# Trading two slots of a streaming ring for two more kept tiles in a two-layer decode kernel

## The chip, the cores and the metric

The kernel runs on one core of one Trainium2 chip; the other cores are idle. The metric is the time of one execution in microseconds (us) as the device measures it. Executions of one kernel agree within about 0.3% for the kernel before and within about 1% for some of the variants below. Ratios are computed as the mean time of one kernel's fast runs over the mean time of the other's fast runs of the same rounds, so they are not quite the ratio of the medians that are quoted.

Engine names are those of the profile: PE (matmul), PEld (PE's weight loads), DVE, ACT, POOL and SP, which issues the DMAs.

## The reference, cut to what matters

Two identical layers with the same weights and the same caches act on a batch of 8 single tokens. Each layer is an attention over a cache of 4096 positions (8 key/value heads, 256 wide, two query heads on each) and then a small MLP block.

```python
q = (layernorm(x) @ wq)                      # 8 tokens, 16 query heads of 256
scores = einsum(q, k_cache) / 16             # k_cache, v_cache: [8, 8, 4096, 256] bf16
o = softmax(scores) @ v_cache
x = x + o @ wo
x = x + B(layernorm(x))                      # gelu MLP, w3: 448 x 1792, w4: 1792 x 448
# ... and the same once more, with the same caches
```

Both caches together are 2 x 128 MiB. Each layer needs all of them, while all that the kernel holds on chip comes to about 26 MiB (206.9 KiB in each of 128 partitions, counted from the code). So nearly every byte has to be streamed twice.

## The kernel before: what the change and the argument touch

The caches are streamed in half tiles of 1 MiB (2048 positions of one head) through a ring of slots, always in the order in which they are used:

```python
N_RING = 6                 # slots of 8 KiB a partition
N_KEEP = 8                 # half tiles of transposed keys that stay, 8 KiB a partition each
...
def load_next():
    n = state["loaded"]
    ...
    t, r = ring[n % N_RING]
    op("sp", lambda e: e.dma_start(t[:, :, :], ...), writes=[r], dma=f"ring{n % N_RING}")
```

`op` records an operation with what it reads and writes and works out the waits: a load waits until the last reader of its slot is done. A keys half tile is turned (16 transposes on PE, evicted by DVE or ACT), and its slot is free then. A values half tile is used by 16 matmuls, after the softmax.

The turned keys of layer 1 can be **kept** on chip. With `N_KEEP = 8`, four of eight heads of a token keep theirs, so layer 2 has to stream only their values. The kept tiles serve one token at a time, so layer 2 of token b runs interleaved with layer 1 of token b + 1:

```python
full = N_KEEP // 2
kept_heads = full + N_KEEP % 2
A  = lambda b: [(0, b, h) for h in range(kept_heads, HKV)]   # layer 1, not kept
Bk = lambda b: [(0, b, h) for h in range(kept_heads)]        # layer 1, kept
C  = lambda b: [(1, b, h) for h in range(kept_heads)]        # layer 2, keys on chip
Dn = lambda b: [(1, b, h) for h in range(kept_heads, HKV)]   # layer 2, all streamed
...
per = (len(first) + len(second)) / B        # first: all A of tokens 1..7, second: all Dn of 0..6
...
for b in range(B):
    ... # about `per` heads out of first and second: the streaming stage S_b
    for i in range(kept_heads):             # the mixed stage M_b
        seq += C(b)[i:i + 1]
        if b + 1 < B:
            seq += Bk(b + 1)[i:i + 1]
```

Between the last kept head of token b in layer 1 (end of stage M) and its first kept head in layer 2 (start of the next M) lies the token's **chain**: output projection, layernorm, MLP, another layernorm, new queries. It has about 370 small matmuls in 46 steps on PE, and some 30 steps on other engines, which depend on each other. The chain is fed into the program in pieces, one or so at each of the 14 **pump** calls of a streamed head; what is left when the first kept head comes is drained at once:

```python
def step():
    ...                                     # records the next piece of the first job
    return 1.0 if len(S.ops["pe"]) > n else 0.4   # 1.0 for a piece with PE work

def pump():
    credit["n"] = min(1.0, credit["n"] + credit["rate"]) if jobs else 0.0
    if credit["n"] > 0.0:
        credit["n"] -= step()
...
    if layer == 0:                          # a token's last head of layer 1 is done
        credit["rate"] = 0.80
        jobs.append(mix(b, 1, True))        # its chain
...
for g, (layer, b, h) in enumerate(seq):
    if layer == 1 and all(s_[:2] != (1, b) for s_ in seq[:g]):
        drain()                             # the chain must be over before layer 2 of token b
    w = attend(g)
```

So a round of the pipeline is: streaming stage S (7 heads of four 1 MiB transfers, with the chain), mixed stage M (four pairs of six transfers, no chain).

## Time and profile before

Two runs: 1195.41 and 1197.05 us, median 1196.23. (The profiled execution is another one, of 1198.42 us.)

These are lines of the page of the kernel before. The digits are 40 equal slices of the span: granted PE clock and DMA busy share in tenths, and GB/s. Then come the shares of the chain that ended last, and the ring's transfers with their number, size and median us from issue to landing.

```profile
span 1196.6 us, 42443 instructions
...
PEclk8879989899999998999989899998999999899886
DMA  9999999999999999999999999999999999999992
GB/s 352 388 412 420 419 416 415 420 419 418 417 421 412 415 403 419 420 419 400 409 420 419 414 401 420 418 421 398 410 420 420 418 407 420 420 419 408 397 393 92
...
DMA 44%; PE 39%; DVE 10%; issue 5%; POOL 1%; ACT 1%; SPq 0%; POOLq 0%; ACTq 0%
...
ring<-in_A_v_cache_dram SPq DMA_DIRECT2D x256, 1024.0 KB, 12.7
ring<-in_A_k_cache_dram SPq DMA_DIRECT2D x192, 1024.0 KB, 12.4
```

The DMA line is full from start to the last slice, and the rate stays near 420 GB/s: the kernel is bound by its stream. A transfer needs 12.5 us to land because it queues behind about four others (12.5 / 2.48 us between landings is 5 under way); the ring is nearly always fully asked for.

The stages can be found in the trace, since each head has exactly one maximum over its scores (a TENSOR_REDUCE into `pm`), in the order of the program; a stage ends with its last head's. These are two rows of the stretch view of the kernel before, for the second streaming stage S1 and the mixed stage M1 (start:end, length, then busy us and number of instructions of each engine, granted clock, DMA share, GB/s):

```profile
core 0: us, PE busy (x) PEld busy (x) DVE busy (x) ACT busy (x) POOL busy (x), PEclk, DMA share, GB/s
244.00:315.90 71.90, 62.12 (x1288) 54.55 (x1280) 34.24 (x127) 21.40 (x57) 6.06 (x16) 1.00 1.01 418
315.90:376.10 60.20, 44.17 (x920) 38.29 (x912) 20.65 (x65) 15.42 (x48) 6.02 (x16) 0.94 1.01 416
```

PE is busy 62 of 72 us in S1, and 44 of 60 in M1: the chain makes S the tight stage for PE, while the stream runs at the same rate in both. And these are lines of the view of waits (engine and line, what it waited for: us in total, times, longest) for PE:

```profile
PE tk L574 <- DMA ring<-in_A_k_cache_dram: 120.4, 81, 6.7
PE ps L598 <- DVE sm L324: 17.6, 20, 1.1
PE mm L405 <- DVE t L364: 13.1, 8, 5.0
PE mm L405 <- DVE lnT L364: 9.1, 1, 9.1
```

PE waits for keys (`tk` is the transposition) more than five times longer than for the layernorms' results (L364 writes them, 13.1 + 9.1 us; the 9.1 us is one wait at the start, for the first queries).

| kernel before | value |
|---|---|
| transfers of 1 MiB | 448 |
| median time between two landings | 2.48 us (423 GB/s) |
| streaming stages S0 to S7, sum | 597.1 us (56 heads; 4 x 2.48 us each would be 555.5) |
| mixed stages M0 to M6, sum | 403.8 us (28 pairs; 6 x 2.48 us each would be 416.6) |

Read the last two rows together: in S, PE falls a little behind the stream and the slots fill with landed data; in M, PE catches up by working off what has landed, so an M takes less than its own transfers' time.

### The profile page before, as it was taken

How to read it: one execution, taken by the hardware profiler on the slowest of the kernel's cores; microseconds unless marked ns; L12 is line 12 of the kernel's file. 1: busy time of each engine (PE TensorE's matmuls, PEld its weight loads, DVE VectorE, ACT ScalarE, POOL GpSimd, SP SyncE). 2: the span in 40 equal slices, each digit the busy share in tenths (PEclk: the TensorE clock that was granted, in tenths of full speed). 3: DMA queues.
4: the chain of work that ended last, by engine and by line, in shares of the span. 5: the costliest groups of instructions: out<-in, count | busy, mean ns of one | idle time of the engine just before them, and what ended most of it. 6: DMA issues, size and time to landing. Idle time of an engine off the chain costs nothing.

```text
span 1196.6 us, 42443 instructions
## 1 busy us (share of the span) xinstructions
PE 963.4 (81%) x19195; PEld 842.2 (70%) x19195; DVE 485.2 (41%) x1707; ACT 320.9 (27%) x907; POOL 104.9 (9%) x281
## 2 busy tenths in 40 slices
PE   2767898788877888788977897788878897789895
PEld 2666787677766777677866886677767786678784
DVE  2323443335433443335433443335433443345253
ACT  1222322232222222232322322222322232223130
POOL 0000001101011001100110001000110011000100
PEclk8879989899999998999989899998999999899886
DMA  9999999999999999999999999999999999999992
GB/s 352 388 412 420 419 416 415 420 419 418 417 421 412 415 403 419 420 419 400 409 420 419 414 401 420 418 421 398 410 420 420 418 407 420 420 419 408 397 393 92
DMA packets 71828, 483.06 MB, mean 404 GB/s; under 512 B 7376, under 2 KB 13408, under 8 KB 13920
## 3 DMA queue, kind: packets, MB, share of 16 engines
q1 hardware_dynamic: 71648, 480.36, 97.9%
q8 instruction: 150, 2.46, 0.8%
q14 instruction: 30, 0.25, 0.0%
HBM read 480.32 MB, written 0.01 MB: 401 GB/s over the span
## 4 chain that ended last, share of the span: by engine, by line
DMA 44%; PE 39%; DVE 10%; issue 5%; POOL 1%; ACT 1%; SPq 0%; POOLq 0%; ACTq 0%
DMA ring<-in_A_k_cache_dram 44%; PE tk L574 21%; PE ps L598 6%; PE pvb L672 4%; PE mm L405 4%; DVE ktr L581 3%; PE mm L485 2%; PE mm L435 1%; PE pvb L690 1%; DVE sm L343 1%; ACT ktr L579 1%; DVE sm L325 1%; POOL gm L648 1%; DVE sm L326 1%; DVE ob L678 1%
## 5 line engine op out<-in xcount | busy, mean ns | idle before, releaser
L574 PE MATMUL tk<-ident,ring 128*128 128x128 f32 x3072 | 458.3, 298 | 121.9 <-DMA ring<-in_A_k_cache_dram 120.4
L574 PEld LDWEIGHTS tk<-ident,ring 128*128 128x128 f32 x3072 | 368.1, 152 | 160.4 <-DMA ring<-in_A_k_cache_dram 147.9
L581 DVE COPY ktr<-tk 128x512 f32<-128x512 f32 x256 | 176.7, 690 | 258.3 <-PE tk L574 257.6
L579 ACT COPY ktr<-tk 128x512 f32<-128x512 f32 x256 | 148.3, 586 | 358.3 <-PE tk L574 358.2
L672 PE MATMUL pvb<-ring,pT 128*2 128x256 bf16 x4096 | 161.7, 279 | 35.9 <-DMA ring<-in_A_v_cache_dram 28.5
L598 PE MATMUL ps<-qT,ktr 128*128 128x48 bf16 x4096 | 145.4, 184 | 22.6 <-DVE sm L324 17.6
L598 PEld LDWEIGHTS ps<-qT,ktr 128*128 128x128 bf16 x4096 | 130.5, 97 | 34.1 <-DVE ktr L581 26.0
L581 DVE COPY keep<-tk 128x512 f32<-128x512 f32 x128 | 88.5, 691 | 155.3 <-PE tk L574 154.7
L654 ACT ACTIVATE pT<-ps,nb 128x32 bf16<-128x32 f32 x256 | 76.4, 298 | 259.3 <-DVE nb L650 212.0
L598 PE MATMUL ps<-qT,keep 128*128 128x48 bf16 x4096 | 139.6, 186 | 5.1 <-issue 4.4
L598 PEld LDWEIGHTS ps<-qT,keep 128*128 128x128 bf16 x4096 | 130.4, 99 | 18.2 <-issue 10.3
L579 ACT COPY keep<-tk 128x512 f32<-128x512 f32 x128 | 75.0, 586 | 232.5 <-PE tk L574 232.5
L672 PEld LDWEIGHTS pvb<-ring,pT 128*2 128x2 bf16 x4096 | 76.0, 82 | 61.0 <-DMA ring<-in_A_v_cache_dram 35.2
L648 POOL PARTITION_ALL_REDUCE gm<-pm x128 | 45.4, 355 | 778.3 <-DVE pm L645 778.3
L678 DVE COPY ob<-pvb 128x256 f32<-128x256 f32 x128 | 53.7, 419 | 46.9 <-PE pvb L672 46.3
L659 POOL PARTITION_ALL_REDUCE dn<-rs x128 | 51.0, 399 | 150.9 <-ACT pT L654 150.9
L645 DVE TENSOR_REDUCE pm<-ps 128x2 f32<-128x64 f32 x128 | 28.6, 224 | 87.8 <-PE ps L598 87.8
L435 PE MATMUL mm<-oT,wo_sb 128*128 128x24 bf16 (+5 forms) x1280 | 60.6, 183 | 1.4 <-DVE oT L697 0.5
L435 PEld LDWEIGHTS mm<-oT,wo_sb 128*128 128x128 bf16 (+1 forms) x1280 | 51.3, 102 | 12.6 <-issue 9.1
L690 PE MATMUL pvb<-ident,ob 128*128 128x128 f32 x256 | 55.8, 302 | 2.8 <-DVE ob L678 1.6
L405 PE MATMUL mm<-lnT,wq_sb 128*128 128x24 bf16 x864 | 48.6, 184 | 10.5 <-DVE lnT L364 9.1
L405 PEld LDWEIGHTS mm<-lnT,wq_sb 128*128 128x128 bf16 x864 | 42.0, 99 | 19.2 <-DVE lnT L364 10.5
(65 smaller groups left out, 474.7 us busy)
## 6 DMA issues: line engine op xcount, KB each, us to landing
ring<-in_A_v_cache_dram SPq DMA_DIRECT2D x256, 1024.0 KB, 12.7
ring<-in_A_k_cache_dram SPq DMA_DIRECT2D x192, 1024.0 KB, 12.4
wo_sb<-in_A_wo_dram SPq DMA_DIRECT2D x1, 3584.0 KB, 26.8
wq_sb<-in_A_wq_dram SPq DMA_DIRECT2D x3, 1024.0 KB, 11.5
w_sb<-in_B_w_dram SPq DMA_DIRECT2D x1, 1568.0 KB, 22.8
w_sb<-in_B_w_dram SPq DMA_DIRECT2D x3, 448.0 KB, 14.3
wqf_sb<-in_A_wq_dram SPq DMA_DIRECT2D x2, 256.0 KB, 15.2
w3f_sb<-in_B_w_dram SPq DMA_DIRECT2D x2, 112.0 KB, 15.3
```

The costliest lines, as they stand in the source:

```text
L405: last = e.matmul(room(P, at + t * B, n), cols(kc, t), copies(rhs, n), start=(kc == 1), stop=(kc == 0), skip_group_check=True)
L435: last = e.matmul(room(w, at, n) if alone else mm[0:w, at:at + n], wo[:, t, row0(c):row0(c) + w], copies(cols, n) if alone else cols, star ...
L574: last = e.transpose(bank[:, j * P:(j + 1) * P], src[:, 4 * (f % 4) + j, :].bitcast(f32), ident4[:, :])
L579: op("act", lambda e: e.copy(flat, bank[:, :]), reads=[r_bank], writes=[r_kt])
L581: op("dve", lambda e: e.tensor_copy(flat, bank[:, :]), reads=[r_bank], writes=[r_kt])
L598: last = e.matmul(pst[:, at:at + 2 * N_REP].rearrange("p (r j) -> p r j", j=2), kt(i, c), repeated(qT[:, b, c, 2 * h:2 * h + 2]), start=(c ...
L648: op("pool", lambda e: e.partition_all_reduce(gm[q][0][:, :], pm[q][0][:, :], P, ReduceOp.max), reads=[pm[q][1]], writes=[gm[q][1]])
L654: return e.activation(pT[q][0][:, :, :].rearrange("p i j -> p j i")[:, j, :], pst[:, C_S:C_S + 2 * NI].rearrange("p (i j) -> p j i", j=2)[ ...
L659: op("pool", lambda e: e.partition_all_reduce(dn[q][0][:, :], rs[q][0][:, :], P, ReduceOp.add), reads=[rs[q][1]], writes=[dn[q][1]])
L672: last = e.matmul(pvb[at:at + 2, 0:DH], pT[q][0][:, a * HALF + i, :], v[:, i, :], start=(a == 0 and i < 4), stop=(a == 1 and i >= HALF - 4 ...
L678: op("dve", lambda e: e.tensor_copy(ob[:, :], pvb[:, 0:DH]), reads=[r_pv], writes=[r_ob])
L690: last = e.transpose(pvb[:, DH + c * P:DH + (c + 1) * P], ob[:, c * P:(c + 1) * P], ident4[:, :])
```

## The change

Its intent is to stream less. Ten half tiles are kept instead of eight, so five heads of eight stream only values in layer 2: 16 key transfers of 448 go away. The memory for it comes from the ring, which shrinks from six slots to four. With five kept heads there are fewer streaming heads a round (`per` falls from 7 to 5.25), so the chain has to fit in 5 or 6 heads; the pump is made denser for it. This is the whole diff:

```diff
-N_RING = 6
+N_RING = 4
 N_KTR = 4
 N_TK = 4
-N_KEEP = 8
+N_KEEP = 10
 N_REP = 24
 N_MLP = 24
+CHAIN = 60
@@ pump
         credit["n"] = min(1.0, credit["n"] + credit["rate"]) if jobs else 0.0
-        if credit["n"] > 0.0:
+        while credit["n"] > 0.0:
             credit["n"] -= step()
@@ after
         if layer == 0:
-            credit["rate"] = 0.80
+            credit["rate"] = CHAIN / (14 * (per - 1))
             jobs.append(mix(b, 1, True))
```

The rate becomes 60 / (14 x 4.25) = 1.008. With `if`, a step of 0.4 (no PE work) takes a pump of its own; with `while`, up to three of them go into one.

## The prediction

> **What bounds the kernel now.** The DMA stream. The page shows the DMA line at 9 tenths in nearly every slice, 480 MB read from HBM, and 404 GB/s over the span; PE is busy 81%. From the issue and landing times of the 448 ring transfers (1 MiB each), one lands every 2.48 us (423 GB/s) whether 2 or 6 are outstanding; about 17 times an interval grows by 1 to 1.5 us, when a few instruction-fetch packets of the second queue come in (about 27 us in all). The Trainium skill, "HBM Reference", section Specifications, gives about 425 GB/s for one core streaming alone, bounded by its 16 DMA engines; the trace agrees, so no rate is left to gain, only bytes. The DMA is busy without a hole from 3 us to about 1140 us; the tail after the last landing (1176 us) is 20 us.
>
> **What the change does.** Two more half tiles kept: 16 fewer K transfers (192 -> 176), 432 instead of 448: 16 x 2.48 = 39.7 us of stream. It also removes 256 transposes (a half tile's 16 take 2.0 us warm, 3.6 cold) and their evictions, off the critical path. Instruction fetches stay. Pure DMA floor: 1196.2 - 39.7 = about 1156.5 us.
>
> **What is given back.**
> 1. Streaming stages. Between the mixed stages the kernel streams 7 heads (K and V), later 5 or 6, and must run the token's dense chain (about 370 matmuls) there. The head-by-head timeline gives: a streamed head without chain, PE-bound, 7.0 us (the last head), against 4 x 2.48 = 9.9 us of DMA; with chain 9.4 to 11 us. So already now PE is a little slower than DMA there, and outstanding transfers fall from 5-6 to 3-4 in each such stage. After, the chain starts in the second of 5 heads. Estimate for the remaining four: 28 + 12 (370 x 33 ns, read from heads with and without chain) + 4 to 9 us of stalls = 44 to 49 us, against 39.7 us of DMA. Stalls now are about 4.5 us a stage (waits for the layernorm's VectorE results); the `while` lets up to three layernorm steps go in one pump, so their latency is covered by fewer transposes: stalls grow.
> 2. Four slots. Waiting PE leaves about 3.3 transfers outstanding instead of 5.3; PE may fall behind by about 5.5 us before the DMA runs dry, against 10 us. So I expect 1 to 4 us of DMA hole in each of six 5-head stages, about none in the two 6-head ones: 10 us (0 to 24).
> 3. Start: during the first projection two fewer chunks are prefetched: 3 us. The last stages, where only 2 or 3 are outstanding now: 2 us.
>
> The mixed stages (PE idle 12 us of 58 on DMA) stay DMA-bound and get longer: 10 heads, about 75 us.
>
> **Prediction.** 1156.5 + 15 = about 1171 us, 8 in 10 between 1157 and 1188. Faster by over 2%: 0.53; within 2%: 0.44; slower: 0.03.
>
> **What would show the steps.** HBM read near 463.5 MB; K transfers x176; time to landing from 12.5 down to about 7.5 us; landing interval still 2.48 us; in the streaming stages GB/s falls from 407-418 to about 390-405 with moments of no transfer outstanding; the page's GB/s line dips there and stays 420 in mixed stages; waits of PE on VectorE's layernorm lines grow, waits on K transfers shrink.
>
> **What would make it wrong.** If the ring absorbs the chain, 1157-1160. If landing intervals stretch with 1 or 2 outstanding, or the denser chain stalls VectorE's evictions, holes of over 5 us a stage eat the whole gain.

## The result

Two runs: 1287.52 and 1294.52 us, median 1291.02, against 1196.23 before. The ratio is 1.079, 95% interval 1.066 to 1.092: slower by 8%. The prediction had been 1171 us, between 1157 and 1188.

The page of the kernel after, the same lines:

```profile
span 1285.7 us, 41851 instructions
...
PEclk8879888898988988898888987898887988889986
DMA  7999989998999989998999989997999989999893
GB/s 278 370 401 406 361 310 408 404 402 304 393 396 393 356 341 402 394 386 318 376 398 400 359 335 396 400 394 283 394 393 377 368 309 386 375 396 335 335 346 128
...
PE 47%; DMA 39%; DVE 8%; issue 4%; POOL 1%; ACT 0%; SPq 0%; POOLq 0%; ACTq 0%
...
ring<-in_A_v_cache_dram SPq DMA_DIRECT2D x256, 1024.0 KB, 8.3
ring<-in_A_k_cache_dram SPq DMA_DIRECT2D x176, 1024.0 KB, 8.0
```

The 16 key transfers are gone, but the GB/s line now has a deep dip in every round (310, 304, 341, 318 ...), and between the dips it reaches about 400, not 420. PE leads the chain that ended last. The stretch view of the same two stages of the kernel after (S1 now has 5 heads, M1 five pairs):

```profile
262.00:324.50 62.50, 49.64 (x1000) 43.64 (x992) 27.25 (x105) 15.65 (x41) 4.57 (x12) 0.92 0.90 353
324.50:401.90 77.40, 58.54 (x1180) 50.84 (x1172) 26.12 (x82) 19.30 (x60) 7.54 (x20) 0.89 0.99 398
```

S1 takes 62.5 us for 5 heads, whose 20 transfers need 49.6. At 353 instead of 418 GB/s the stage moved 22.1 MB where 26.1 were possible: 9.7 us of stream lost. M1 runs at 398 instead of 416 GB/s, another 3.3 us lost, although PE has 19 us to spare in it. And the view of waits:

```profile
PE tk L575 <- DMA ring<-in_A_k_cache_dram: 142.8, 79, 7.2
PE mm L406 <- DVE lnT L365: 40.1, 10, 11.1
PE mm L406 <- DVE t L365: 31.1, 9, 5.0
PE mm L486 <- DVE hT L477: 9.2, 10, 1.2
```

PE now waits 71 us for the layernorms' results (40.1 + 31.1) where it waited 22 (9.1 + 13.1), and it waits longer for keys too.

| | before | after |
|---|---|---|
| transfers | 448 | 432 |
| S0 to S7, sum | 597.1 us, 56 heads | 528.5 us, 42 heads (4 x 2.48 us each: 416.6) |
| M0 to M6, sum | 403.8 us, 28 pairs | 551.2 us, 35 pairs (6 x 2.48 us each: 520.8) |
| first 8 heads | 110.3 us | 119.8 us |
| last 8 heads and the tail | 85.4 us | 86.2 us |
| landings, median and mean time between two (between 95 us and 60 us before the last) | 2.48, 2.55 us | 2.49, 2.84 us |
| share of these over 2.7 us | 6% | 34% |

So the loss is spread over both stages. Two theories were held against each other. **R**: the ring is too short; four slots cannot keep the stream going. **C**: the chain is packed too densely; it stalls PE, and any ring would run dry. All runs below are correct by the comparison with the reference unless said otherwise.

### The profile page after: what moved, and what is told of

It reads as the page before. It is cut to its first block, busy times and chain, and to the rows that moved or that the text cites. A ratio compares the mean times of both kernels' runs of the same rounds, so it can differ in the third digit from the quotient of the medians.

```text
span 1285.7 us, 41851 instructions
## 1 busy us (share of the span) xinstructions
PE 981.9 (76%) x18939; PEld 862.0 (67%) x18939; DVE 473.6 (37%) x1675; ACT 306.0 (24%) x875; POOL 105.1 (8%) x281
## 3 DMA queue, kind: packets, MB, share of 16 engines
HBM read 463.54 MB, written 0.01 MB: 361 GB/s over the span
## 4 chain that ended last, share of the span: by engine, by line
PE 47%; DMA 39%; DVE 8%; issue 4%; POOL 1%; ACT 0%; SPq 0%; POOLq 0%; ACTq 0%
DMA ring<-in_A_k_cache_dram 39%; PE tk L575 25%; PE ps L599 8%; PE pvb L673 4%; PE mm L406 4%; PE mm L436 2%; PE pvb L691 2%; DVE ktr L582 2%; PE mm L486 1%; DVE sm L326 1%; DVE sm L327 1%; DVE sm L344 1%; DVE sm L325 1%; POOL sm L340 1%; DVE xc L358 0%
## 5 line engine op out<-in xcount | busy, mean ns | idle before, releaser
L575 PEld LDWEIGHTS tk<-ident,ring 128*128 128x128 f32 x2816 | 372.8, 164 | 181.4 <-DMA ring<-in_A_k_cache_dram 170.7
L582 DVE COPY ktr<-tk 128x512 f32<-128x512 f32 x192 | 132.5, 690 | 205.9 <-PE tk L575 205.6
L580 ACT COPY ktr<-tk 128x512 f32<-128x512 f32 x192 | 112.6, 586 | 344.8 <-PE tk L575 344.8
L582 DVE COPY keep<-tk 128x512 f32<-128x512 f32 x160 | 110.5, 691 | 226.2 <-PE tk L575 225.8
L599 PE MATMUL ps<-qT,keep 128*128 128x48 bf16 x5120 | 177.7, 188 | 10.2 <-issue 6.3
L599 PEld LDWEIGHTS ps<-qT,keep 128*128 128x128 bf16 x5120 | 167.4, 100 | 26.0 <-issue 13.8
L580 ACT COPY keep<-tk 128x512 f32<-128x512 f32 x160 | 93.7, 586 | 355.0 <-PE tk L575 355.0
L599 PE MATMUL ps<-qT,ktr 128*128 128x48 bf16 x3072 | 114.2, 188 | 0.7
L599 PEld LDWEIGHTS ps<-qT,ktr 128*128 128x128 bf16 x3072 | 103.3, 100 | 4.8 <-ACT ktr L580 1.7
L691 PE MATMUL pvb<-ident,ob 128*128 128x128 f32 x256 | 61.7, 329 | 0.8 <-DVE ob L679 0.8
## 6 DMA issues: line engine op xcount, KB each, us to landing
w_sb<-in_B_w_dram SPq DMA_DIRECT2D x1, 1568.0 KB, 16.5
```

The lines of the kernel that those rows point to most:

```text
L575: last = e.transpose(bank[:, j * P:(j + 1) * P], src[:, 4 * (f % 4) + j, :].bitcast(f32), ident4[:, :])
L580: op("act", lambda e: e.copy(flat, bank[:, :]), reads=[r_bank], writes=[r_kt])
L582: op("dve", lambda e: e.tensor_copy(flat, bank[:, :]), reads=[r_bank], writes=[r_kt])
L599: last = e.matmul(pst[:, at:at + 2 * N_REP].rearrange("p (r j) -> p r j", j=2), kt(i, c), repeated(qT[:, b, c, 2 * h:2 * h + 2]), start=(c ...
L691: last = e.transpose(pvb[:, DH + c * P:DH + (c + 1) * P], ob[:, c * P:(c + 1) * P], ident4[:, :])
```

## The experiments

### The three parts of the change one by one, and the ring put back

Run `e1_ring4_only` is the kernel before with four slots.

```diff
-N_RING = 6
+N_RING = 4
```

> The kernel before with four ring slots instead of six and nothing else changed (8 half tiles kept, old pump, 448 ring transfers). Theory R (the ring: with at most 4 transfers asked for, the stream loses its rate whenever PE falls behind or one DMA engine lags after an instruction fetch): 1245 to 1280 us, mean about 380 GB/s, landing intervals over 2.6 us in far more than 10% of the transfers, also in the mixed stages. Theory C (the chain: packed into fewer heads by the new pump it stalls PE, and the ring hardly matters): 1196 to 1215 us.

Run `e2_pump_only` is the kernel before with the new pump.

```diff
-        if credit["n"] > 0.0:
+        while credit["n"] > 0.0:
...
-            credit["rate"] = 0.80
+            credit["rate"] = 60 / (14 * (per - 1))
```

> The kernel before with the new pump alone (while instead of if, rate 60/(14 x 6) = 0.714), six slots, 8 kept. Theory R: 1193 to 1206 us, since the chain still has 7 heads and six slots absorb the longer waits for the layernorm. Theory C: 1220 us or more; waits of PE on the layernorm's lnT grow to 3 us and more a stage, as in the kernel after.

Run `e3_old_pump` is the kernel after with the old pump.

```diff
-        while credit["n"] > 0.0:
+        if credit["n"] > 0.0:
...
-            credit["rate"] = CHAIN / (14 * (per - 1))
+            credit["rate"] = 0.80
```

> The kernel after with the old pump (one step at most per pump, rate 0.80), four slots and 10 kept. The chain then does not fit into 5 heads and a rest of it (about 15 of its PE steps, or a layernorm) is drained at once before the first kept head. Theory R: 1275 to 1310 us, about as slow as the kernel after. Theory C, if it is the while that stalls PE: 1240 us or less.

Run `e4_ring6_keep10` is the kernel after with six slots. To make room for two more slots, `wo` and `w4` are allocated at half size and hold only half of their tiles; their other halves are loaded over the first, so that the bytes are the same.

```diff
-N_RING = 4
+N_RING = 6
...
-    wo, r_wo = sb("wo_sb", [P, 32, D], bf)
+    wo, r_wo = sb("wo_sb", [P, 16, D], bf)      # used as wo[:, t % 16, ...]
-    w4, r_w4 = sb("w4_sb", [P, NF, D], bf)
+    w4, r_w4 = sb("w4_sb", [P, NF // 2, D], bf) # used as w4[:, t % 7, ...]
```

> The kernel after with six slots, made room for by keeping wo and w4 at half size (all their bytes are still loaded, in two parts, one over the other; the result is wrong on purpose, and the instructions are the same). Theory R: 1165 to 1195 us, at or below the kernel before, outstanding transfers 3 to 5, landing interval back at 2.48 us in the mixed stages. Theory C: 1255 us or more.

| run | median us | ratio to before (95%) |
|---|---|---|
| e1_ring4_only | 1262.4 | 1.057 (1.054 to 1.059) |
| e2_pump_only | 1202.9 | 1.006 (1.004 to 1.007) |
| e3_old_pump | 1263.8 | 1.056 (1.052 to 1.059) |
| e4_ring6_keep10 | 1203.8 | 1.006 (1.005 to 1.008) |

The ring alone costs 66 us in the kernel before, as theory R had it; the pump alone costs 7. And yet PE waits 67 us for layernorm results in `e2_pump_only` (40.6 + 26.8), nearly as long as in the kernel after (71): with six slots and 7 heads a stage such waits cost little, so the sum of the waits is not what was lost. The run with the ring put back gains 87 us on the kernel after (the half-size weights have a part in this, see the control below). But it does not come down to 1165 to 1195 us, so R is not all of it: with six slots the 16 saved transfers still bring nothing. And with the old pump the kernel after is 27 us faster than with its own: C has a part. The expectation for `e3_old_pump` (1275 to 1310) was too slow.

The stretch views show who does what. First S1 and M1 of `e1_ring4_only`, then S1 and M1 of `e4_ring6_keep10`:

```profile
257.60:333.60 76.00, 64.94 (x1288) 57.39 (x1280) 34.24 (x127) 21.61 (x57) 6.06 (x16) 0.96 0.99 391
333.60:394.90 61.30, 45.66 (x924) 39.29 (x915) 20.57 (x65) 15.42 (x48) 6.02 (x16) 0.92 1.01 410
```

```profile
242.40:304.70 62.30, 50.22 (x1000) 44.83 (x996) 27.19 (x106) 15.56 (x41) 4.56 (x12) 0.89 0.96 383
304.70:373.70 69.00, 55.95 (x1176) 48.66 (x1172) 25.92 (x82) 19.27 (x60) 7.53 (x20) 0.93 1.00 415
```

With six slots S1 still takes 62.3 us: in a 5-head stage with the dense pump **PE sets the pace, whatever the ring**. The ring decides what the stream does meanwhile (383 against 353 GB/s), and how fast M goes afterwards (69.0 against 77.4 us). Summed over S0 to S7, six slots take 515.8 us against 528.5 with four; over M0 to M6, 493.5 against 551.2. With four slots and 7 heads, S1 is only 4 us longer than before, but the rate falls below 415 in both stages. Over all rounds, the step from six to four slots in the kernel before cost 11 us in S (597.1 to 608.5) and 43 us in M (403.8 to 446.6).

### Why four slots are too few: the stream by itself

The prediction had reckoned with a transfer every 2.48 us as long as any is outstanding. Two runs measure the stream alone: 1 MiB key transfers into a ring, each slot released after a number of transposes, one phase for each pair of slots and transposes (each ran once, at a mean granted clock of 0.99). Their outputs are wrong, which doesn't matter for the times.

```python
PHASES = [(1, 1, 24), (2, 1, 40), (3, 1, 48), (4, 1, 56), (6, 1, 64),   # slots, transposes, transfers
          (3, 16, 48), (4, 16, 56), (6, 16, 64)]
```

> A stream alone (result wrong on purpose): 1 MiB key transfers through 1, 2, 3, 4 and 6 slots, each slot released by a single transpose; then through 3, 4 and 6 slots, each released by 16 transposes (about 2 us of hold warm, 3.6 cold). Theory L (a transfer keeps its slot for about 2.4 us beyond its 2.45 us of data, before the data start and after they end, so a slot's cycle is 4.9 us plus hold): landing every 5.2 to 5.6 us with 1 slot, 2.6 to 2.9 with 2, 2.48 with 3, 4 and 6; with 16 transposes 2.5 to 3.0 with 3 slots, 2.48 with 4 and 6. Theory D (few outstanding transfers are slow by themselves, because the DMA engines get out of step): 4 slots stay above 2.6 us even with the short hold.

The stretch view of `m1_slots`, one row for each phase in this order (last number GB/s; the number of slots is not in the line):

```profile
11.70:135.70 124.00, 10.46 (x22) 4.02 (x22) 0.00 (x0) 0.00 (x0) 1.00 0.55 186
147.00:255.50 108.50, 17.59 (x37) 6.74 (x37) 0.00 (x0) 0.00 (x0) 1.00 0.97 357
266.00:376.60 110.60, 20.93 (x44) 8.03 (x44) 0.00 (x0) 0.00 (x0) 1.00 1.01 419
389.00:515.80 126.80, 24.25 (x51) 9.30 (x52) 0.00 (x0) 0.00 (x0) 1.00 1.01 422
533.60:676.50 142.90, 27.07 (x57) 10.38 (x57) 0.00 (x0) 0.00 (x0) 1.00 1.01 422
687.80:823.20 135.40, 91.18 (x703) 82.66 (x704) 0.00 (x0) 0.00 (x0) 0.95 0.93 341
837.60:965.80 128.20, 100.28 (x816) 88.21 (x816) 0.00 (x0) 0.00 (x0) 1.00 1.01 421
983.20:1126.30 143.10, 112.06 (x912) 98.58 (x912) 0.00 (x0) 0.00 (x0) 1.00 1.00 414
```

With one slot, a transfer is issued, its first data move 0.96 us later, its last data land 3.7 us after that, and the semaphore comes 0.35 us later still: 5.04 us from issue to landing, against 2.48 us between landings when the stream is full. So **a transfer occupies its slot about 2.6 us longer than the stream needs for its bytes**. The Trainium skill agrees in part, in "DMA: Bandwidth & Descriptors", section "Anatomy of one DMA — SWDGE (gpsimd) path": a DMA costs a fixed part of about 2.0 us plus its bytes at 436 GB/s (an estimate from these figures: 4.4 us for 1 MiB), and the fixed part is mostly completion latency. That is for DMAs issued from POOL; here they are issued from SP, take 5.04 us, and only 0.35 us of it comes after the last data.

A slot's cycle is then 5.04 us plus the time that it is held by its reader. Four slots at the full rate have 4 x 2.48 = 9.92 us for it, which leaves 4.9 us of hold; six slots leave 9.8. The runs bear it out: three slots (7.44 us) are enough for a hold of 0.6 us (419 GB/s), but not for one of 2.1 us (341 GB/s), although 5.04 + 2.1 = 7.1 us would just fit. There the transfers took 7.1 us to land (median), so the time of a lone one is a lower bound, and a sum that just fits is too tight; what makes them longer was not taken apart. Theory D, that few outstanding transfers are slow by themselves, falls: four slots with a steady hold reach 421 GB/s.

But the holds in the kernel are not steady. In the mixed stages of `e1_ring4_only`, the slot of a first keys half is held 3.5 us on average (3.8 us in the worst tenth), the values behind it 2.9, others 0.9 to 2.5. (A hold is the time from the landing to the next issue into the slot.) The second run alternates long and short holds, of 4 slots, then 5 and 6:

```python
PHASES = [(4, (16, 16), 48), (4, (22, 10), 64), (4, (28, 4), 64), (4, (32, 4), 64),
          (5, (32, 4), 64), (6, (32, 4), 64)]
```

> A stream alone (result wrong on purpose), slots released by an uneven number of transposes, about 18 on average: with 4 slots 16 and 16, then 22 and 10, 28 and 4, 32 and 4 (the longest hold about 4.1 us, as a cold PE's in the mixed stages); then 32 and 4 with 5 and with 6 slots. Theory L (a slot's cycle is 5 us plus hold, and 4 slots at 2.48 us each leave 4.9 us): 2.49 us for the first two, 2.55 to 2.9 us for 28 and 4 and for 32 and 4 with 4 slots, 2.49 to 2.52 with 5 and 6. If uneven holds don't matter: 2.49 us everywhere, and the loss in the mixed stages has another cause.

The stretch view of `m2_holds`, one row for each phase in this order:

```profile
15.60:123.80 108.20, 84.55 (x688) 74.39 (x688) 0.00 (x0) 0.00 (x0) 1.00 1.01 421
136.30:285.00 148.70, 113.68 (x950) 104.22 (x950) 0.00 (x0) 0.00 (x0) 0.99 1.01 416
297.50:452.30 154.80, 112.62 (x939) 106.23 (x940) 0.00 (x0) 0.00 (x0) 0.97 0.99 402
465.90:630.40 164.50, 125.69 (x1067) 119.29 (x1068) 0.00 (x0) 0.00 (x0) 0.98 0.97 378
645.90:792.30 146.40, 121.17 (x1054) 114.29 (x1053) 0.00 (x0) 0.00 (x0) 1.00 1.01 419
810.60:953.60 143.00, 119.39 (x1037) 112.76 (x1038) 0.00 (x0) 0.00 (x0) 1.00 0.99 411
```

Four slots fall from 421 to 378 GB/s when every other hold grows from 2.1 to 3.8 us, and a fifth slot brings nearly all of it back. (Mean times between landings, the first four and last six of each phase left out: 2.49, 2.53, 2.62, 2.78 us with four slots, 2.50 with five and with six; the 411 of the last row is the end of the run, in which no transfer follows.) The short holds shrink only to 1.8 us, as PE still has the other slot's transposes to do, so the mean hold grows as well, from 2.1 to 2.8 us. How much is due to the unevenness and how much to the longer mean was not separated; what is shown is that holds of up to 3.8 us are too long for four slots, though 5.04 + 3.8 = 8.8 us would fit into 9.92. The mixed stages of `e1_ring4_only` (378 to 410 GB/s) and of the kernel after (379 to 400) lie in the same range.

There may be a loop in it. PE's granted clock is 1.0 or 0.5 in this trace; a half tile's 16 transposes take 2.0 us at the full clock and 3.6 us at half. The Trainium skill, "TensorE: Matmul & The Clock Gate", Part 1, says that the clock is halved after an idle window of about 3.4 us. The trace agrees: in S1 of the kernel after, PE waits 3.58 us, and the granted clock is 0.5 from 312.9 to 319.8 us (the wait is shown in the next section). When the stream has a hole, PE waits, cools and holds the next slot longer, which makes the next hole. PE spent 182 us at half clock before, 253 us in `e1_ring4_only` and 360 us after. That PE runs cold is seen; how much of the loss the loop itself makes, if any, was not taken apart.

### What the dense chain costs: four lines of the timeline

The timeline of the kernel after in S1, cut to PE's transposes and the end of one layernorm (start, length, engine and line; in brackets the idle time before, and what ended it):

```profile
308.93 0.66 PE L575 MATMUL tk<-ident,ring 128*128 128x128 f32 x4
...
312.94 0.18 DVE L365 TENSOR_TENSOR lnT<-xc,sm 128x4 bf16<-128x4 f32 x1
...
313.17 0.26 PE L406 MATMUL mm<-lnT,wq_sb 128*128 128x24 bf16 x3 [3.58 <-DVE lnT L365]
...
314.80 1.09 PE L575 MATMUL tk<-ident,ring 128*128 128x128 f32 x4
```

The layernorm's steps on DVE and POOL take from 307.6 to 313.1 us and depend on each other. The old pump spread them over nine pumps, behind which PE had transposes and scores to do. The new one puts up to three in a pump, so that PE comes to the first matmul that needs `lnT` 3.58 us too early. After this wait, four transposes take 1.09 us instead of 0.66: the clock has been halved. In S1 the waits for `t`, `lnT` and `hT` come to 7.9 us, against 4.4 us (waits for `t`, `sm` and `hT` and a few more) before.

### Six slots with the old pump; smaller slots; no chain

Run `e5_ring6_keep10_oldpump` is `e4_ring6_keep10` with the old pump (the diff of `e3_old_pump`).

> Six slots, ten kept (wo and w4 at half size as in the run with six slots and the new pump), old pump. If the chain has no room in 5 heads whichever pump runs it: 1180 to 1210 us, streaming stages of about 54 us for 5 heads, and the rest of the chain drained in the first mixed heads. If it was the while that cost the time: below 1170 us.

Run `e7_halfslots` is the kernel after with its 32 KiB of ring cut into eight slots of 512 KiB transfers.

```diff
-N_RING = 4
+N_RING = 8
-    ring = [sb(f"ring{i}", [P, HALF, DH], bf) for i in range(N_RING)]
+    ring = [sb(f"ring{i}", [P, HALF // 2, DH], bf) for i in range(N_RING)]
 ... # two loads and two releases where there was one
```

> The kernel after with the same 32 KiB of ring cut into eight slots of 512 KiB transfers instead of four of 1 MiB. Theory L (fixed time per transfer plus hold; a slot of half the size is held half as long and the ring is refilled in finer steps): 1230 to 1265 us, mixed stages back near 410 GB/s, streaming stages still bound by PE. If only the bytes in flight count, or smaller transfers cost more: 1280 us or more.

Runs `e8_nochain_ring4` and `e9_nochain_ring6` are the kernel after, with four and with six slots (half-size weights), without the tokens' chains between the layers. Their outputs are wrong, which doesn't matter for the times.

```diff
         if layer == 0:
             credit["rate"] = CHAIN / (14 * (per - 1))
-            jobs.append(mix(b, 1, True))
```

> The kernel after without the chains of the single tokens between the layers (layer 2 uses the first queries; result wrong on purpose), four slots. What the ring alone costs at 432 transfers: 1190 to 1215 us, streaming stages of 5 heads at 50 to 53 us, mixed stages as in the kernel after (about 395 GB/s). If the chain was all of the loss: 1160 us or less.

> Ten kept, six slots (wo and w4 at half size) and no chain between the layers (result wrong on purpose): the stream of 432 transfers with neither of the two suspects. Theory: it is the floor of the prediction, 1150 to 1165 us. If it stays above 1175 us, a third cause eats the gain (kept heads, cold PE, the ends).

| run | median us | ratio to before (95%) |
|---|---|---|
| e5_ring6_keep10_oldpump | 1186.7 | 0.991 (0.989 to 0.994) |
| e7_halfslots | 1273.8 | 1.064 (1.062 to 1.066) |
| e8_nochain_ring4 | 1192.6 | 0.997 (0.994 to 1.000) |
| e9_nochain_ring6 | 1140.6 | 0.953 (0.951 to 0.955) |

(`e8_nochain_ring4` had a slow run, 1214.8 us, among its five; it is left out of the median, and it is the profiled one, so its profile is not used here.)

The two runs without a chain are the cleanest test. Without the chain and with six slots, the saving is there in full, and both S1 and M1 of `e9_nochain_ring6` go at nearly the full rate:

```profile
238.40:288.80 50.40, 35.65 (x662) 31.30 (x650) 19.36 (x50) 15.52 (x40) 3.76 (x10) 1.00 1.01 426
288.80:363.90 75.10, 57.90 (x1152) 50.62 (x1140) 25.70 (x80) 19.30 (x60) 7.53 (x20) 0.89 1.01 422
```

Without the chain but with four slots, the kernel is as slow as the one before: **the ring alone eats the whole gain, even with the chain out of the way**. And the chain alone, at six slots, eats it too: `e5_ring6_keep10_oldpump` is hardly faster than the kernel before. Its S1 and M1 in the stretch view:

```profile
241.50:297.50 56.00, 46.68 (x903) 40.81 (x891) 24.38 (x89) 15.44 (x41) 4.58 (x12) 0.94 1.01 419
297.50:374.90 77.40, 60.96 (x1269) 53.68 (x1269) 28.32 (x98) 19.31 (x60) 7.56 (x20) 0.87 0.93 383
```

The old pump lets S1 go in 56.0 us at 419 GB/s, but does not finish the chain in 5 heads; the rest is drained at the start of M1, where PE waits for a layernorm with nothing behind it (the instructions of PE move from S1 to M1: 903 against 1000, 1269 against 1176), and M1 falls to 383 GB/s. The new pump pays in S, the old one in M.

### A control of the half-size weights

The six-slot runs with ten kept landed a transfer every 2.43 to 2.44 us, where the others need 2.48. Run `c1_before_halfweights` gives the kernel before the same half-size weights and changes nothing else.

> Control: the kernel before with wo and w4 at half size, all bytes loaded as before (result wrong on purpose). If the half-size weights, by moving the ring in memory, make the stream faster by themselves: landing interval 2.43 us and about 1175 us. If not: 2.48 us and 1194 to 1199 us, and the faster interval of the six-slot runs has another cause.

It took 1185.6 us (ratio 0.991, 0.989 to 0.992), with a landing every 2.44 us. So the half-size weights alone make the stream faster, by 10.7 us in this kernel, and the runs made with them must be compared with this control: `e5_ring6_keep10_oldpump` (1186.7) then gains nothing, `e4_ring6_keep10` (1203.8) loses 18 us, and `e9_nochain_ring6` gains 45 (no run has the kernel before without its chain, so these 45 us are the saved transfers and the missing chain together). Taking the 10.7 us out as an estimate, the parts of the change are these (medians, us):

| | six slots | four slots |
|---|---|---|
| 8 kept, old pump | 1196.2 | 1262.4 |
| 8 kept, new pump | 1202.9 | not run |
| 10 kept, old pump | 1186.7, without the bias about 1197 | 1263.8 |
| 10 kept, new pump | 1203.8, without the bias about 1214 | 1291.0 |
| 10 kept, no chain (wrong result) | 1140.6, without the bias about 1151 | 1192.6 |

In every row with two numbers, four slots cost 41 to 77 us. From row to row, ten kept with the chain bring nothing in either column. With ten kept and the new pump, the chain costs 63 us with six slots and 98 with four, the short ring 41 us without the chain and 77 with it: neither is the one cause, and each makes the other dearer. The comparison with the reference did not see half of `wo` and `w4` being wrong: in simulated values this changes the output by 0.3%. "Correct" is therefore weak evidence for changes in that part.

Why the landings come faster with half-size weights stays open. The 8 KiB packets take 309 ns throughout then, and up to 321 ns otherwise. Placing the ring ahead of the weights in memory is not it (run `c2_v1_ringfirst`, below).

### A version from the findings

If four slots are too few and five enough, and the chain is what makes the 5-head stages too long, then nine kept half tiles with five slots and a lighter chain should win something: 440 transfers, a floor of 1196.2 - 8 x 2.48 = 1176 us. Run `v1_early_ring5_keep9` is the kernel after with two further changes: three quarters of a token's output projection are done as soon as six of its eight heads are done, in the mixed stage, where PE waits for the stream anyway; and a pump does 1.3 steps of PE work or one step of any other kind, so the layernorm is again spread out. `v2_early_ring4_keep10` is the same with four slots and ten kept.

```diff
-N_RING = 4
+N_RING = 5
-N_KEEP = 10
+N_KEEP = 9
...
     def pump():
-        credit["n"] = min(1.0, credit["n"] + credit["rate"]) if jobs else 0.0
-        while credit["n"] > 0.0:
-            credit["n"] -= step()
+        credit["n"] = min(credit["rate"], credit["n"] + credit["rate"]) if jobs else 0.0
+        while credit["n"] > 0.0 and jobs:
+            if step() == 1.0:
+                credit["n"] -= 1.0
+            else:
+                credit["n"] = 0.0
...
+    def early(b, ts):
+        for c in (1, 2, 3, 0):
+            for n in range(0, len(ts), 8):
+                outputs(b, 1, c, ts[n:n + 8], c == 1 and n == 0, False)
+                yield
...
+        if layer == 0:
+            done_heads[b].append(h)
+            if len(done_heads[b]) == HKV - 2:
+                jobs.append(early(b, [t for t in range(32) if t // 4 in done_heads[b]]))
...
-            credit["rate"] = CHAIN / (14 * (per - 1))
-            jobs.append(mix(b, 1, True))
+            credit["rate"] = 1.3
+            jobs.append(mix(b, 1, True, rest=[t for t in range(32) if t // 4 in done_heads[b][-2:]]))
```

The split sum needs care. The Trainium skill, "PSUM — Partial Sum Buffer", section "Terms", says that the first matmul of a group clears the accumulation bits of its whole 2 KiB bank, in the quadrants of partitions that it writes; so only the first of all these matmuls may start a group (`c == 1 and n == 0`), and none of the others, the late two heads included. No run tests what another order would do. Simulated values of this version equal those of the kernel before bit for bit.

> The same relieved chain with five slots and nine half tiles kept (440 transfers, floor 1196 - 8 x 2.48 = 1176 us): 1176 to 1195 us, mixed stages at 410 GB/s and more.

> The kernel after (four slots, ten kept) with the chain relieved: the output projection of a token's first six heads runs early, in the mixed stage, where PE waits for DMA; and a pump does 1.3 steps of PE work or a single other step. Streaming stages of 5 heads fall from about 63 to 53 to 56 us, mixed stages stay at about 78 us as four slots hold them: 1200 to 1225 us. If the chain's density was not what filled the streaming stages: above 1260 us.

Four controls tell what its gain comes from: the lighter chain with six slots and eight kept; five slots and nine kept with the old pump and chain; the kernel before with five slots; and the new version with its ring in ten slots of 512 KiB. A fifth places its ring ahead of the weights. Their diffs are `N_RING` and `N_KEEP`, the slots of `e7_halfslots`, and one line moved.

> The kernel before (six slots, eight kept) with the relieved chain. Its stream was already without a hole, so nothing is to be won: 1190 to 1198 us. If the relieved chain is what made the run with nine kept faster: 1186 us or less.

> Five slots, nine kept, old pump and old chain: eight transfers fewer, but the chain does not fit in 5 heads: 1200 to 1230 us. If the saved transfers alone made the faster run: 1190 us or less.

> The kernel before with five slots. By the stream alone (2.51 us with five slots at the longest holds, against 2.80 with four) the mixed stages keep the full rate, but PE may fall less far behind in the streaming stages: 1198 to 1215 us, far nearer to the six-slot time than to the 1262 us of four.

> Nine kept, relieved chain, and the memory of five slots cut into ten slots of 512 KiB: finer release lets more bytes be outstanding: 1178 to 1186 us. If the smaller transfers cost as much as they give: 1187 us or more.

> The fastest version so far (five slots, nine kept, relieved chain) with the ring allocated ahead of the weights. If the ring's place sets the 2.43 us: about 1166 us. If it does not matter: 1182 to 1192 us.

| run | slots, kept | chain | median us | ratio to before (95%) |
|---|---|---|---|---|
| v1_early_ring5_keep9 | 5, 9 | lighter | 1186.8 | 0.992 (0.988 to 0.996) |
| v2_early_ring4_keep10 | 4, 10 | lighter | 1229.7 | 1.026 (1.020 to 1.031) |
| v3_early_ring6_keep8 | 6, 8 | lighter | 1196.6 | 1.000 (0.998 to 1.001) |
| v4_oldpump_ring5_keep9 | 5, 9 | old | 1237.5 | 1.034 (1.032 to 1.036) |
| e10_ring5_keep8 | 5, 8 | old | 1207.4 | 1.008 (1.006 to 1.010) |
| v5_v1_halfslots | 10 of 512 KiB, 9 | lighter | 1211.7 | 1.012 (1.011 to 1.014) |
| c2_v1_ringfirst | 5, 9 | lighter | 1189.6 | 0.994 (0.991 to 0.997) |

(`v2_early_ring4_keep10` had a slow run, 1239.1 us, among its four; it is left out.) The new version is the fastest correct one with whole weights, by 0.8%, which is within 2% of the kernel before. Its stages S1 and M1:

```profile
243.90:299.70 55.80, 45.98 (x936) 40.35 (x924) 27.02 (x107) 15.61 (x41) 4.56 (x12) 0.94 1.00 402
299.70:377.50 77.80, 60.61 (x1264) 53.22 (x1252) 26.90 (x82) 20.34 (x62) 7.53 (x20) 0.93 1.01 417
```

M1 is back at 417 GB/s with five slots, and S1 takes 55.8 us instead of 62.5. PE's waits for `lnT` and `t` fall from 71 to 35 us (18.6 + 16.5). Of the 19.8 us of transfers that it saves, 9.8 are left against the control with eight kept (`v3_early_ring6_keep8`). The controls say that both parts are needed: the lighter chain alone changes nothing where the stream has no holes, and five slots with nine kept lose 41 us with the old chain, which then spills into the mixed stages. The lighter chain is two changes, the early projection and the new pump rule, and these were not taken apart. Five slots cost 11 us in the kernel before, four 66.

The clearest separation is `v2_early_ring4_keep10` against the kernel after: slots and kept tiles are the same and only the chain is lighter. It takes 61 us less. S0 to S7 fall from 528.5 to 463.2 us, while M0 to M6 stay (551.2 and 554.8 us). So the dense chain filled the streaming stages, and the four slots slow the mixed ones. Its S1 and M1:

```profile
247.90:302.50 54.60, 43.91 (x930) 38.78 (x923) 26.89 (x108) 15.62 (x41) 4.56 (x12) 1.00 0.99 397
302.50:381.90 79.40, 60.37 (x1234) 52.71 (x1226) 25.79 (x81) 19.27 (x60) 7.53 (x20) 0.89 0.98 387
```

Smaller slots help where the ring is too short (`e7_halfslots`, 17 us off the kernel after) and hurt where it is not (`v5_v1_halfslots`, 25 us more). These are the lines of packets on the pages of `v1_early_ring5_keep9` and `v5_v1_halfslots`:

```profile
DMA packets 70675, 474.66 MB, mean 399 GB/s; under 512 B 7248, under 2 KB 13280, under 8 KB 13792
```

```profile
DMA packets 134041, 474.73 MB, mean 392 GB/s; under 512 B 14288, under 2 KB 20320, under 8 KB 133472
```

Half a slot is 4 KiB a partition instead of 8, and nearly all packets are below 8 KiB then. A packet of 4 KiB takes 160 ns and one of 8 KiB 309 ns (medians), so two small ones take 320: landings of 512 KiB come every 1.28 us, which is 2.56 for 1 MiB. On a stream of 440 MiB the 0.08 us are 35 us (an estimate); `v5_v1_halfslots` lost 25. That the finer steps gained the rest back is not shown.

Expectations that missed, beside those named: `e7_halfslots` (1230 to 1265 expected) and `v2_early_ring4_keep10` (1200 to 1225) were slower, `v4_oldpump_ring5_keep9` (1200 to 1230) and `v5_v1_halfslots` (1178 to 1186) too, `e9_nochain_ring6` was faster than its range (the half-size weights); the control `c1_before_halfweights` fell between its two, and `m1_slots` landed a little slower than its ranges with one slot (5.63 us), with two (2.93) and with three held long (3.1).

## Why the prediction was wrong, point by point

The stream's floor was right. What failed is what is given back: 15 us were predicted on a floor of 1156.5, and about 134 came.

- **What bounds the kernel before, and what is removed: right.** The bytes (463.54 MB, 463.5 predicted), the 176 key transfers and the 39.7 us of stream are as predicted, and `e9_nochain_ring6` shows that the stream gets shorter when nothing disturbs it. "No rate is left to gain" was not right: with half-size weights the same stream landed every 2.44 us (430 GB/s).
- **"PE may fall behind by about 5.5 us before the DMA runs dry": this step failed.** It counted 3.3 outstanding transfers as stock worth 2.48 us each, less about one. A transfer takes 5.04 us from issue to landing even on an idle stream, 2.6 us of it beyond the full stream's pace, so with four slots most of the cycle is used up by transfer and hold (5.04 + 3.5 = 8.5 of 9.92 us for a first keys half). The first transfer of the trace before had said so: issued at 1.2 us, landed at 6.3. Predicted were 1 to 4 us of hole in a 5-head stage; S1 lost 9.7 us. About 5 of these (an estimate: 62.3 us at 383 instead of 418 GB/s) are lost with six slots too (`e4_ring6_keep10`), so they are the chain's and not the ring's.
- **"Landing interval still 2.48 us", and mixed stages "stay DMA-bound ... about 75 us": failed, and this is most of what the ring cost.** The median stayed (2.49), but 34% of the intervals are over 2.7 us and the mean is 2.84; the mixed stages take 77.2 to 81.0 us at 379 to 400 GB/s, and they no longer catch up what S lost. Four slots with alternating holds of up to 3.8 us did not run at the full rate in the stream alone either (2.78 us). The ring alone cost 66 us in the kernel before; by the profiled runs 43 of it fell in M and 11 in S, and with ten kept 58 in M and 13 in S (`e4_ring6_keep10` against the kernel after, the half-size weights included). The prediction gave the ring 10 us (0 to 24), all of it in S.
- **"44 to 49 us" for the four heads with the chain: the mechanism was right, the size was not.** The four heads of S1 took 52.7 us (271.8 to 324.5). Waits grew to 7.9 us a stage, within the 4 to 9 reckoned with, but the halved clock after the two long ones was left out: PE ran 10.2 us of the four heads at half the clock, which is up to 5 us (an estimate), and in the last head of S1 the granted clock is 0.75. Over all rounds this is the other large part: with the lighter chain of `v2_early_ring4_keep10`, S takes 65 us less.
- **Start 3 us, ends 2 us:** the first eight heads took 9.5 us longer, the last ones 1.
- The last sentence of the prediction named the case that came ("if landing intervals stretch ... or the denser chain stalls ..."), yet gave slower by over 2% a chance of 0.03. What was missing was a look at how long a lone transfer takes.

## What to carry to other kernels

In these runs a streaming ring needed clearly more slots than (time to landing of a lone transfer + longest usual hold) / (time between landings): three slots were enough where this gave 2.3 and four where it gave 2.9, but three were too few at 2.9 and four at 3.6, where five nearly did. Before memory is taken from a ring, read the time to landing of the very first transfer and the holds from the trace; the count of outstanding transfers in the steady state is no measure of the stock. A saving on the bottleneck is worth nothing in a stage where something else, here a dependent chain squeezed into fewer heads, takes over as the bottleneck, so move that work to where its engine idles first.

## What the Trainium skill lacked or had wrong

- "DMA: Bandwidth & Descriptors" has the fixed cost of a DMA, but not what it means for a ring: how many transfers must be outstanding. Here, with 1 MiB transfers: 186 GB/s with one slot, 357 with two, 419 with three at a hold of 0.6 us; 341 with three and 421 with four at a hold of 2.1 us; 378 with four and 419 with five at alternating holds of 3.8 and 1.8 us.
- The same page fits the fixed cost to DMAs issued from POOL, and gives about 0.6 us to the first byte for those issued from SP. The latter agrees: 0.96 us from the start of the issuing instruction to the first data, 0.33 us of it the instruction itself, so 0.63 us from its end. The fixed cost does not carry over as a latency at the end: from the last data to the landing it is 0.35 us, while a lone 1 MiB transfer moves its data in 3.7 us, not in the 2.48 us between landings of a full stream.
- The same page puts the smallest transfer for the full rate at 512 bytes (section "Specifications"); packets of 4 KiB, at 160 ns, were still a little slower than those of 8 KiB, at 309 ns: 2.56 against 2.48 us for 1 MiB in the landings.
- No page says why the same stream lands 1 MiB every 2.44 us in one kernel and every 2.48 us in another that differs in the size of two weight tensors (1185.6 and 1196.3 us). These runs don't tell either.
